# Attention beside the plain passes, last w1's factors, half loads and staging moved in a fused attention and mixture-of-experts kernel

## The chip, the cores and the metric

The kernel runs on one core of one Trainium2 chip. The metric is the device time of one execution in microseconds (us); for a kernel it is the median of its runs. Beside the runs one further execution is profiled, and its trace is what the views of the profile show. In them PE is TensorE (matmuls; PEld its weight loads), DVE is VectorE, ACT is ScalarE, POOL is GpSimd, SP is SyncE, which issues all DMAs here.

## The reference

Inputs are q, k, v of shape (8, 8, 576, 64): batch, heads, sequence, head size. In each chunk of 64 positions softmax attention is computed; the result is the input x of four experts. All is fp32.

```python
scores = scale * np.matmul(q_c, k_c.transpose(0, 1, 2, 4, 3))     # per chunk of 64
attn = np.exp(scores - max); attn = attn / (sum + 1e-09)
x = (attn @ v_c) as (4608 tokens, 512)
p = domain_probs / (domain_probs.sum(-1, keepdims=True) + 1e-09)   # (4608, 4)
for e in range(4):
    h = np.maximum(x @ w1[e], 0.0)       # w1[e]: 512 x 1024
    out += p[:, e:e + 1] * (h @ w2[e])   # w2[e]: 1024 x 512
```

## The kernel before, in words

**Products.** Every fp32 product is three matmuls on parts: a matrix is split into a high part (a cast on ACT, `hi_part` L361) and a low part (what is left, a subtraction on POOL or DVE, `lo_part` L364), and hi x hi, hi x lo, lo x hi are summed in PSUM (`product`, L638). A large matmul is 128 x 128 by 512 columns.

**Passes.** An expert's hidden layer is cut in halves, which gives 8 passes over the weights. The 4608 tokens are a first block of 512 and four pairs of 2 x 512. The first block goes through `startup` (pass 0) and the plain passes 1 to 7; pair 0 through passes 8 to 15, pair 1 through 16 to 23, and so on to 39. A plain pass (`plain_pass`) has 8 steps of 12 matmuls: four hidden steps (`plain_hidden`, its relu on ACT L645 and its low part on DVE L646) and four tiles of the output (`whole`). The last step of pass 7 is held and runs in pass 8.

**Factors.** The passes of the pairs multiply 2 x 2 blocks with seven products instead of eight. Their left factors are the weights' blocks a11, a12, a22 and four sums s1 to s4 (`Factors.sum`, L415), each split into two parts (`make`). The plain passes make the factors of w1 and w2 for the pass they run and store them in DRAM (`keep`, L424 for a sum; `keep_quad`, `keep_unit` for blocks). `w1_split` and `w2_split` split the blocks; these splits the plain products use themselves. The first w1's sums are made in passes 1 to 5 (`FIRST_W1`), the last w1's (that of pass 7) in pass 7 and stored in pass 8. The right factors are x's blocks b11, b21, b22 and sums t1 to t4 (`Tokens`, L588).

**Woven passes.** `first_later_pass` (pass 8) has 14 steps, `later_pass` 28 steps of 6 matmuls in the order of `WOVEN`: a and b are the outer products of the pass before (w2), g and h the hidden ones of this pass (w1), by output half. Products accumulate into banks A, B, C of PSUM; ACT copies one aside (`keep`, L701), DVE adds (L836, and L863 into the output sums `acc`). The relu times the probability is on DVE (L801), sums of the hidden parts on DVE and POOL (L807), the casts and low parts on ACT (L813) and POOL (L816). Each product reads a unit of factors, which `ring_load` brings from DRAM into one of the tiles `wf0` to `wf5` (L536) three units ahead (`ring_next`).

**Factors made later.** For w1 of passes 9 to 14 the stored units don't exist yet when pair 0 needs them: `half_load` (L484) loads half of a w1's raw columns into `xraw`, `half_sum` (L489, DVE) forms s1 to s4 there, and `make` casts on ACT (L501), subtracts on POOL (L502) straight into the ring tile and stores the unit for the later pairs (L505). The places of the makes in a pass are `MAKE_AT`. For the last w2 (used in passes 15 and 16) the sums are formed in pass 7 and stored raw (`keep_sums`); `raw_load` (L525) brings a unit of raw blocks or sums back into the one tile `v_in`, and `make` works from there.

**Attention.** Pair 0's attention (8 tiles of 128 tokens, five steps each, one more to begin) runs beside the plain passes: `Beside.go` is called in each step and issues attention steps at a rate of 41 over 37 per step, so that sometimes two come in one. A tile is: scores on PE (L161), less the maximum (DVE), exp (ACT L243), sums and scaling (DVE), transposes (DVE), copies that place the weights (ACT L194, and four small L198), products with v (PE L208), copies into `xraw` (ACT L223, L224). Pair 1's attention is placed by `TILES` into passes 9 to 14, at the steps `EARLY` and `LATE`: weights, place, values.

**Order.** The kernel fixes the order by hand: each engine works through its instructions in the order in which the program issues them. `add(at, i, f)` puts f behind step i of the pass; `first` is a list issued ahead of `at` in the same step. SP issues DMAs in the same way, and a DMA that has to wait holds those behind it.

## Time and profile before

| quantity | value |
|---|---|
| median of 3 runs | 1523.31 us (1521.61 to 1524.45) |
| the profiled execution | 1522.23 us |
| its span, first to last instruction | 1520.5 us |
| TensorE clock granted, mean over the span | 0.995 |
| instructions | 23324 |
| DMA bytes | 345.89 MB, mean 227 GB/s |

How to read it: the page gives each engine's busy time and share of the span. A row of the timeline has the start and the length in us, the engine, the line, the operation, what is written and read (buffer numbers left out), and in brackets the idle time before it with what ended it. A row of the waits reads: the waiting engine, tile and line, the releaser, then the sum in us, the count and the longest. A row of the windows gives, for a stretch of the span, each engine's busy time with its instructions in brackets, then the granted clock (1.00 is full speed). SPq is SP's queue of DMA issues.

### The profile page before, as it was taken

To read this page: it belongs to the slowest core of one execution; us is meant where nothing else is said; L and a number is where in the kernel's file an instruction comes from. 1 tells how busy PE (TensorE), PEld (TensorE's weight loads), DVE (VectorE), ACT (ScalarE), POOL (GpSimd) and SP (SyncE) were. 2 spreads that over 40 slices of the span, in tenths; PEclk is the share of its full clock that TensorE was granted. 3 is DMA by queue.
4 is the path that set the end of the run, shared out by engine and by line. 5 is a ranking of instruction groups with operands and counts; after the bars stand their busy time and mean duration, and the time that the engine had idled before them with its cause. 6 is when DMAs were issued, how large, how long until landed. Compare 5 with 4: busy or idle time off the path is not lost.

```text
span 1520.5 us, 23324 instructions
## 1 busy us (share of the span) xinstructions
PE 1475.2 (97%) x8556; PEld 1203.5 (79%) x8556; DVE 1081.8 (71%) x1500; ACT 626.2 (41%) x1165; POOL 964.6 (63%) x720
## 2 busy tenths in 40 slices
PE   8999997999999989999999999999999999999998
PEld 7777876777777867888888888888888888888887
DVE  5566664778887786777776886777777966666665
ACT  4546633545445343434343434343343433333332
POOL 4656995777777776555555765555557655555554
PEclk9999999999999999999999999999999999999999
DMA  8778876776766758866666678666665696565655
GB/s 300 243 237 299 305 263 241 237 255 229 249 212 232 271 192 235 277 206 232 213 216 199 200 222 258 229 209 228 209 200 192 199 252 210 193 208 193 207 194 152
DMA packets 199010, 345.89 MB, mean 227 GB/s; under 512 B 69984, under 2 KB 111216, under 8 KB 198000
## 3 DMA queue, kind: packets, MB, share of 16 engines
q1 hardware_dynamic: 198896, 344.40, 68.8%
q8 instruction: 68, 1.11, 0.3%
q14 instruction: 46, 0.38, 0.1%
HBM read 272.97 MB, written 71.38 MB: 226 GB/s over the span
## 4 chain that ended last, share of the span: by engine, by line
PE 61%; DMA 1%; DVE 0%; ACT 0%; POOL 0%; SPq 0%; issue 0%; DVEq 0%; ACTq 0%
PE A L638 34%; PE C L638 17%; PE B L638 8%; PE psa L208 1%; PE psa L161 1%; DMA out<-pt 0%; DMA v_in<-w_sums 0%; DVE acc L863 0%; DVE wraw L807 0%; ACT pt L198 0%; POOL wf L502 0%; POOL hf L816 0%; DVE pt L971 0%; PE C L1596 0%; PE psa L638 0%
## 5 line engine op out<-in xcount | busy, mean ns | idle before, releaser
L816 POOL TENSOR_TENSOR hf<-wraw,hf 128x512 fp32r<-128x512 f32 x384 | 506.6, 1334 | 247.3 <-ACT hf L813 245.0
L638 PE MATMUL A<-hf,wf 128*128 128x512 f32 x1536 | 394.5, 392 | 14.1 <-DMA wf<-w 5.4
L638 PE MATMUL A<-xh,wf 128*128 128x512 f32 (+1 forms) x1104 | 382.3, 390 | 3.8 <-ACT s L701 3.2
L813 ACT CAST hf<-wraw 128x512 fp32r<-128x512 f32 x384 | 234.7, 622 | 303.8 <-DVE wraw L807 99.5
L638 PEld LDWEIGHTS A<-hf,wf 128*128 128x128 f32 x1536 | 286.4, 188 | 80.8 <-DVE acc L863 11.1
L638 PEld LDWEIGHTS A<-xh,wf 128*128 128x128 f32 x1104 | 207.3, 188 | 48.9 <-ACT s L701 4.1
L701 ACT COPY s<-A 128x512 f32<-128x512 f32 x192 | 112.9, 588 | 279.2 <-PE A L638 278.9
L638 PE MATMUL A<-xl,wf 128*128 128x512 f32 (+1 forms) x552 | 214.2, 389 | 0.0
L863 DVE TENSOR_TENSOR acc<-A,acc 128x512 f32<-128x512 f32 x232 | 158.0, 681 | 76.1 <-PE A L638 75.2
L638 PE MATMUL C<-xh,wf 128*128 128x512 f32 (+1 forms) x600 | 205.7, 390 | 3.6 <-DVE B L836 2.9
L638 PE MATMUL C<-hf,wf 128*128 128x512 f32 x768 | 195.1, 389 | 1.0 <-POOL wf L502 0.6
L638 PEld LDWEIGHTS C<-hf,wf 128*128 128x128 f32 x768 | 144.0, 188 | 31.6 <-POOL wf L502 1.1
L807 POOL TENSOR_TENSOR wf<-wraw,wf 128x512 f32<-128x512 f32 x31 | 40.1, 1293 | 155.9 <-DVE wf L801 155.9
L638 PEld LDWEIGHTS C<-xh,wf 128*128 128x128 f32 x600 | 111.5, 188 | 28.7 <-DVE B L836 4.2
L638 PE MATMUL B<-xh,wf 128*128 128x512 f32 (+1 forms) x376 | 124.8, 383 | 0.0
L863 DVE TENSOR_TENSOR acc<-C,acc 128x512 f32<-128x512 f32 x120 | 82.7, 689 | 53.6 <-PE C L638 44.0
L638 PEld LDWEIGHTS A<-xl,wf 128*128 128x128 f32 x552 | 103.8, 188 | 21.1
L638 PE MATMUL C<-xl,wf 128*128 128x512 f32 (+1 forms) x300 | 114.7, 386 | 0.0
L816 POOL TENSOR_TENSOR hf<-wf,hf 128x512 fp32r<-128x512 f32 x64 | 91.9, 1436 | 33.7 <-ACT hf L813 33.3
L807 DVE TENSOR_TENSOR wraw<-wf,wraw 128x512 f32<-128x512 f32 x64 | 92.7, 1448 | 10.2 <-POOL hf L816 9.0
L638 PE MATMUL B<-hf,wf 128*128 128x512 f32 x384 | 97.7, 389 | 0.8 <-POOL hf L816 0.8
L807 POOL TENSOR_TENSOR wraw<-wraw 128x512 f32<-128x512 f32 x64 | 91.9, 1437 | 0.0
(175 smaller groups left out, 1951.3 us busy)
## 6 DMA issues: line engine op xcount, KB each, us to landing
wf<-w SPq DMA_DIRECT2D x399, 512.0 KB, 4.2
w<-wf SPq DMA_DIRECT2D x49, 512.0 KB, 3.0
qk_in<-in_qk SPq DMA_DIRECT2D x32, 512.0 KB, 4.8
w<-hf SPq DMA_DIRECT2D x28, 512.0 KB, 5.8
w<-hf SPq DMA_DIRECT2D x50, 256.0 KB, 5.4
hf<-in_w SPq DMA_DIRECT2D x7, 1024.0 KB, 5.5
wf<-in_w SPq DMA_DIRECT2D x12, 512.0 KB, 7.6
ws<-p_t SPq DMA_DIRECT2D x24, 256.0 KB, 4.1
```

The lines of the kernel that those rows point to most:

```text
L161: nc.tensor.matmul(s["sc"][of_half(half), c, slot], lhsT=q, rhs=k, start=True, stop=True)
L208: nc.tensor.matmul(av[of_half(slot % 2), half, head // 2], lhsT=s["v"][of_half(half), head], rhs=s["pt"][of_half(half), c, slot], start=Tr ...
L638: nc.tensor.matmul(out, lhsT=lhs(k, a), rhs=rhs(k, b), start=first and i == 0, stop=last and i == len(parts) - 1, skip_group_check=not (fi ...
L701: nc.scalar.copy(out=t, in_=self.a)
L807: (eng or nc.vector).tensor_tensor(out=self.values[place, k], in0=self.values[a, k], in1=self.values[b, k], op=op)
L813: nc.scalar.copy(out=self.part(name, 0)[:, k], in_=self.values[name, k])
L816: (eng or nc.gpsimd).tensor_tensor(out=self.part(name, 1)[:, k], in0=self.values[name, k], in1=self.part(name, 0)[:, k].bitcast(F32), op=A ...
L863: nc.vector.tensor_tensor(out=acc[key], in0=src, in1=acc[key], op=ALU.add)
```

## The change

- **Attention beside the plain passes.** `go` issues one attention step per plain step; the second of all comes ahead of the last tile of the startup.
- **Last w1.** Its raw blocks are loaded in pass 1 into `xh4` and `xl4`, which hold x's parts later; its sums are formed on DVE in passes 3 and 4, its factors made in passes 4 and 5 and stored in 5 and 6 (`EARLY_W1`, which also moves the first w1's by up to a pass). Pass 7 makes and pass 8 stores nothing of it.
- **Pass 1 to 7.** w2's splits come one step later, its sums at steps 3, 3, 4, 5, its load at step 6. Of pass 6's four w2 factors two are made in pass 7. x's sums and parts, before in passes 5 to 7, are spread otherwise over them; sum t4 and its low part go from DVE to POOL, in pass 7.
- **Half loads and half sums.** The first half load for pass 9 goes out in pass 7 (before in pass 8), the second in step 9 of pass 8; in passes 9 to 13 they go out at steps 5, 13 and 19 instead of 10 and 18. Half sums move with them. One make moves from step 9 to step 10.
- **Staging.** The raw units of the last w2 are staged in four buffers in turn (`v_in`, `e`, `pt`, and `s4`, which the probabilities used alone), first in first out.

The diff, cut to its core:

```diff
-    def half_load(n, g):
+    def half_load(n, g, fs=(0, 1)):
...
+        for f in fs:
...
-        src = staged.pop() if i else pieces(2 * k, 2)
+        src = staged.pop(0) if i else pieces(2 * k, 2)
...
-    def raw_load():
-        k, t = unstaged.pop(0), load.tile([P, 2, 2, P], F32, name="v_in")
+    def raw_load(pool, name):
+        k, t = unstaged.pop(0), pool.tile([P, 2, 2, P], F32, name=name)
...
-        def __init__(self, pair, n, close):
+        def __init__(self, pair, close):
             self.steps = attention(pair, close)
-            self.rate, self.due = (5 * PAIR * NT + 1) / n, 0.5
-        def load(self):
+        def go(self):
             next(self.steps, None)
-        def go(self):
-            self.due += self.rate
-            while self.due >= 1.0:
-                self.due -= 1.0
-                next(self.steps, None)
...
-        add(at, 2, lambda: w2f[n - 1].keep(1))
+        add(at, 4 if last_pass else 2, lambda: w2f[n - 1].keep(1))
         for i, (k, f) in enumerate(QUADS):
-            add(at, i // 2, lambda f=f, k=k: w2_split(f, k))
+            add(at, 1 + i // 2, lambda f=f, k=k: w2_split(f, k))
         if n == 2:
             add(at, 1, probs_by_expert)
             add(at, 5, transpose_probs)
         add(at, 0, lambda: w2_factors(n))
+        for i, f in EARLY_W1.get(n, ()):
+            add(at, i, f)
         if not last_pass:
+            near = n == n_pass - 2
             add(at, 0, lambda: w1_load(n + 1))
-            for name, i, eng in zip(SUMS, (1, 2 if n == n_pass - 2 else 3, 3, 4), SUMS_ON.get(n, (v,) * 4)):
+            for name, i, eng in zip(SUMS, (3, 3, 4, 5), (v, g, g, g) if near else (v,) * 4):
                 add(at, i, w2_do("sum", name, eng))
             for i, quad in enumerate(KEPT):
-                add(at, 3 + i // 2, lambda quad=quad: keep_quad(n, *quad))
+                add(at, 4 + i // 2, lambda quad=quad: keep_quad(n, *quad))
             for i, (f, k) in enumerate(QUADS):
                 add(at, (3, 4, 4, 5)[i], lambda f=f, k=k: w1_split(f, k, g))
-            for name, i in zip(("s1", "s2", "s4", "s3"), (4, 5, 6, 7)):
+            for name, i in zip(("s1", "s2", "s4", "s3")[: 2 if near else 4], (6, 7) if near else (4, 5, 6, 7)):
                 add(at, i, w2_do("make", name))
-            add(at, 5, lambda: w2_load(n + 1))
-            for i, f in FIRST_W1.get(n, ()):
-                add(at, i, f)
+            add(at, 6, lambda: w2_load(n + 1))
             if n == n_pass - 3:
-                add(at, 5, lambda: xs.append(Tokens(0)), x("sum1"))
-                add(at, 6, x("sum3"))
-                add(at, 6, x("hi", "t1"))
-                add(at, 7, x("lo", "t1"))
-            if n == n_pass - 2:
-                add(at, 0, x("hi", "b22"))
-                add(at, 0, x("lo", "b22"))
-                add(at, 3, x("sum2"), x("hi", "t3"))
-                add(at, 4, x("lo", "t3"), x("hi", "t2"))
-                add(at, 5, x("lo", "t2"))
-                add(at, 6, x("sum4"))
-                add(at, 7, x("hi", "t4"))
+                add(at, 7, lambda: xs.append(Tokens(0)), x("sum1"))
+            if near:
+                add(at, 0, x("sum3"), x("hi", "t1"))
+                add(at, 3, x("lo", "t1"), x("hi", "b22"))
+                add(at, 4, x("lo", "b22"))
+                add(at, 5, x("sum2"), x("hi", "t3"))
+                add(at, 6, x("lo", "t3"))
+                add(at, 7, x("hi", "t2"))
             issue(steps, at, beside, True)
             return None
-        w1f = Factors(0, n, {
-            name: lambda: wpool.tile([P, 2, 2 * P], F32, name="wraw", bufs=N_RAW) for name in ("s1", "s2")
-        })
-        last_w1.append(w1f)
-        places = []
-        def place(i):
-            if i % 2 == 0:
-                places.append(hf_tile(3 + 3 * (i // 2), (2, 2, *UNIT[1:])))
-            return places[-1][:, i % 2]
-        def w1_make(i, name):
-            return lambda: w1f.make(name, place(i))
         add(at, 0, *(lambda quad=quad: keep_unit(n, *quad) for quad in KEPT))
-        add(at, 0, lambda: w1f.sum("s1", v), lambda: w1f.sum("s2", v))
-        add(at, 1, x("lo", "t4"))
-        add(at, 2, w1_make(0, "s1"), w1_make(1, "s2"))
-        add(at, 3, x("hi", "b11"), x("lo", "b11"), lambda: w1f.sum("s3", v))
-        for name, i in zip(SUMS, (2, 2, 3, 3)):
+        add(at, 0, x("lo", "t2"))
+        for name in ("s4", "s3"):
+            add(at, 2, lambda name=name: w2f[n - 1].make(name))
+        for name, i in zip(SUMS, (2, 2, 5, 6)):
             add(at, i, w2_do("sum", name, g))
-        add(at, 4, x("hi", "b21"), x("lo", "b21"), lambda: w1f.sum("s4", v))
-        add(at, 5, w1_make(2, "s3"), w1_make(3, "s4"))
+        add(at, 3, x("hi", "b11"), x("lo", "b11"))
+        add(at, 3, x("sum4", g))
+        add(at, 4, x("hi", "b21"), x("lo", "b21"))
+        add(at, 4, x("hi", "t4"), x("lo", "t4", g))
         for r, i in ((2, 2), (0, 3), (1, 3), (5, 5), (3, 6), (4, 6)):
             add(at, i, lambda r=r: ring_load(0, r, (RINGS[0] + RINGS[1])[r]))
-        add(at, 4, lambda: probs_load(n + 1, 0), lambda: probs_load(n + 1, 1))
-        add(at, 6, w2_do("keep_sums"))
-        add(at, 6, lambda: first_load(1))
+        add(at, 5, lambda: probs_load(n + 1, 0), lambda: probs_load(n + 1, 1))
+        add(at, 6, lambda: first_load(1), w2_do("keep_sums"), lambda: half_load(n + 2, 0))
         issue(steps[:-1], at, beside, True)
...
+    def last_begin():
+        for k, name in enumerate(("xh4", "xl4")):
+            t = xpool.tile([P, 2, HF], F32, name=name)
+            nc.sync.dma_start(out=t, in_=of_pass(w1, n_pass - 1)[:, 2 * k : 2 * k + 2])
+            for f in range(2):
+                raw[0, f, k] = t[:, :, f * 2 * P : (f + 1) * 2 * P]
+        last_w1.append(Factors(0, n_pass - 1, sums_tile("xh3")))
...
+    EARLY_W1 = {
+        1: [(6, early_sum(first_w1, "s1")), (7, early_sum(first_w1, "s2")), (6, last_begin)],
         2: [
+            (6, early_sum(first_w1, "s3")), (7, early_sum(first_w1, "s4")),
+            (7, early_make(first_w1, "s1", "xl2")),
         ],
+        3: [
+            (0, early(first_w1, "keep", "s1")), (6, early_sum(last_w1, "s1")), (7, early_sum(last_w1, "s2")),
+            (6, early_make(first_w1, "s2", "xh6")), (7, early_make(first_w1, "s3", "xl6")),
+        ],
+        4: [
+            (0, early(first_w1, "keep", "s2")), (1, early(first_w1, "keep", "s3")),
+            (6, early_sum(last_w1, "s3")), (7, early_sum(last_w1, "s4")),
+            (6, early_make(first_w1, "s4", "xh5")), (7, early_make(last_w1, "s1", "xl3")),
+        ],
+        5: [
+            (0, early(first_w1, "keep", "s4")), (1, early(last_w1, "keep", "s1")),
+            (5, early_make(last_w1, "s2", "xl5")), (6, early_make(last_w1, "s3", "xl2")),
+            (7, early_make(last_w1, "s4", "xh6")),
+        ],
+        6: [
+            (0, early(last_w1, "keep", "s2")), (0, early(last_w1, "keep", "s3")),
+            (1, early(last_w1, "keep", "s4")),
+        ],
...
-        add(at, 0, lambda: half_load(n + 1, 0), lambda: half_load(n + 1, 1))
-        for name in ("s1", "s2"):
-            add(at, 0, lambda name=name: last_w1[0].keep(name))
-        for name in ("s3", "s4"):
-            add(at, 2, lambda name=name: last_w1[0].keep(name))
-        half_sums(at, 0, (4, 4, 6, 6))
+        add(at, 9, lambda: half_load(n + 1, 1))
+        half_sums(at, 0, (6, 7, 8))
         add(at, 6, lambda: make_next(0))
+        add(at, 10, lambda: make_next(0))
...
-    MAKE_AT = 2, 9, 11, 14, 17, 20, 24
+    MAKE_AT = 2, 10, 11, 14, 17, 20, 24
...
-            add(at, 10, lambda: half_load(n + 1, 0))
-            add(at, 18, lambda: half_load(n + 1, 1))
-            half_sums(at, 0, (15, 16, 22, 22))
-            half_sums(at, 1, (22, 24))
+            add(at, 5, lambda: half_load(n + 1, 0))
+            add(at, 13, lambda: half_load(n + 1, 1, (0,)))
+            add(at, 19, lambda: half_load(n + 1, 1, (1,)))
+            half_sums(at, 0, (15, 15, 22, 22))
         if n_pass < n < 2 * n_pass - 1:
-            places = zip(SUMS, (9, 9, 10, 10)) if n == n_pass + 1 else (("s3", 9), ("s4", 10))
-            for name, i in places:
-                first.setdefault(i, []).append(lambda name=name: half_sum(1, name))
-            for i in (0, 3, *MAKE_AT[1:]) if n == n_pass + 1 else MAKE_AT:
-                first.setdefault(i, []).append(lambda: make_next(0))
+            half_sums(first, 1, (9, 9, 10, 12))
+            if n == n_pass + 1:
+                half_sums(first, 0, (None, None, None, 3))
+            for i in MAKE_AT:
+                add(first if i == 24 else at, i, lambda: make_next(0))
         for m, makes, raws in (
-            (2 * n_pass - 1, (22, 26), (19, 23, 27)), (2 * n_pass, (2, 8, 12, 15, 20), (4, 9, 13, 16)),
+            (2 * n_pass - 1, (20, 27), ((8, load, "v_in"), (22, att, "e"), (23, att, "pt"), (24, load, "v_in"))),
+            (2 * n_pass, (2, 10, 12, 17, 20), ((1, hpool, "s4"), (12, load, "v_in"), (13, hpool, "s4"))),
         ):
             if n == m:
                 for i in makes:
-                    first.setdefault(i, []).append(lambda: make_next(1))
-                for i in raws:
-                    add(at, i, raw_load)
+                    add(at, i, lambda: make_next(1))
+                for i, *place in raws:
+                    add(at, i, lambda place=place: raw_load(*place))
...
-        beside = Beside(0, (n_pass - 4) * 2 * NK + 5, True)
+        beside = Beside(0, True)
```

Where instructions stand, at three places. First ScalarE at the start of plain pass 1, before: `hf_614` is the raw w2, `A`, `B` and the first `hf` are the hidden step's bank and parts, `psa` and `pt` belong to the attention.

```order
L645 ACTIVATE hf_748<-A_749 128x512
L361 CAST hf_766<-hf_614 128x2x256 x2
L645 ACTIVATE hf_748<-A_778 128x512
L243 ACTIVATE psa<-psa 128x2x256
L361 CAST hf_794<-hf_614 128x2x256 x2
L645 ACTIVATE hf_807<-B_808 128x512
L645 ACTIVATE hf_807<-B_826 128x512
L194 COPY pt<-psa 128x512
L198 COPY pt<-psa 32x8x32 x4
```

The same place after, where all lines of the code stand four lower:

```order
L641 ACTIVATE hf_751<-A_752 128x512
L243 ACTIVATE psa<-psa 128x2x256
L641 ACTIVATE hf_751<-A_780 128x512
L357 CAST hf_796<-hf_614 128x2x256 x2
L641 ACTIVATE hf_801<-B_802 128x512
L194 COPY pt<-psa 128x512
L198 COPY pt<-psa 32x8x32 x4
L357 CAST hf_825<-hf_614 128x2x256 x2
L641 ACTIVATE hf_801<-B_830 128x512
```

The four casts that split w2 stand one relu later, and the copies that place the weights stand a relu earlier, now ahead of the second pair of casts.

Second SyncE in pass 8, before: `w_0_k` is a unit of w1's factors in DRAM, `w_1_k` one of w2's, `hf_2362` and `hf_2437` hold the last w1's factors, `wf` is a ring tile.

```order
L424 DMA w_0_1_196<-hf_2362 128x512
L424 DMA w_0_4_199<-hf_2362 128x512
L536 DMA wf_2494<-w_0_6_103 128x1024
L939 DMA out<-acc_527 128x512
L424 DMA w_0_2_197<-hf_2437 128x512
L424 DMA w_0_5_200<-hf_2437 128x512
L424 DMA w_0_3_198<-hf_2437 128x512
L424 DMA w_0_6_201<-hf_2437 128x512
L505 DMA w_0_0_111<-wf_2574 128x1024
L536 DMA wf_2584<-w_1_0_104 128x1024
```

After, from the last store of the w2 sums on:

```order
L464 DMA w_sums<-acc_2466 128x512
L480 DMA xraw<-in_w 128x4x128 x2
L532 DMA wf_2497<-w_0_6_103 128x1024
L935 DMA out<-acc_527 128x512
L501 DMA w_0_0_111<-wf_2570 128x1024
L532 DMA wf_2580<-w_1_0_104 128x1024
L532 DMA wf_2605<-w_1_1_105 128x1024
L480 DMA xraw<-in_w 128x4x128 x2
```

The eight stores of the last w1 are gone from here. Before, both half loads stood ahead of the first row shown; now the first stands behind the w2 sums, still in pass 7, and the second behind w2's second unit (`w_1_1`).

Third ScalarE in pass 10, around step 9, before: `wf` from `xraw` is a make's cast, `s` a product copied aside.

```order
L701 COPY s_3202<-A_3104 128x512
L501 CAST wf_3208<-xraw 128x2x256
L194 COPY pt<-psa 128x512
L198 COPY pt<-psa 32x8x32 x4
L501 CAST wf_3238<-xraw 128x2x256
L223 COPY xraw<-psa 128x2x2x64
L224 COPY xraw<-psa 128x2x2x64
L243 ACTIVATE psa<-psa 128x2x256
```

After:

```order
L697 COPY s_3203<-A_3103 128x512
L194 COPY pt<-psa 128x512
L198 COPY pt<-psa 32x8x32 x4
L497 CAST wf_3226<-xraw 128x2x256
L223 COPY xraw<-psa 128x2x2x64
L224 COPY xraw<-psa 128x2x2x64
L497 CAST wf_3273<-xraw 128x2x256
L243 ACTIVATE psa<-psa 128x2x256
```

Each of the two makes stands behind the attention's copies that it stood ahead of.

65 lines of the change are left out of this document (27 added, 38 removed).

## The prediction

> **What bounds the kernel now.** I read the page first, then the busy time by stage, then TensorE's waits stage by stage, then the rows around each wait. The page:
>
> ```profile
> span 1520.5 us, 23324 instructions
> PE 1475.2 (97%) x8556; PEld 1203.5 (79%) x8556; DVE 1081.8 (71%) x1500; ACT 626.2 (41%) x1165; POOL 964.6 (63%) x720
> ```
>
> TensorE (PE) is the bound and idles 45.3 us, so only idle time, or matmuls that run slowly, can be won. The change adds and drops no matmul. Where the idle time lies, by stage (us of the stretch, then busy time of each engine):
>
> ```profile
> core 0: us, PE busy (x) PEld busy (x) DVE busy (x) ACT busy (x) POOL busy (x), PEclk, DMA share, GB/s
> 0.00:44.00 44.00, 40.05 (x458) 32.76 (x462) 23.04 (x45) 19.32 (x38) 23.27 (x24) 1.00 0.73 259
> 44.00:196.00 152.00, 144.63 (x1076) 117.87 (x1068) 98.84 (x136) 84.14 (x171) 107.23 (x78) 0.98 0.78 273
> 196.00:219.00 23.00, 19.85 (x86) 15.80 (x85) 15.96 (x14) 9.51 (x15) 22.92 (x15) 1.00 0.80 298
> 219.00:252.00 33.00, 25.30 (x99) 20.15 (x98) 14.51 (x21) 9.18 (x16) 16.66 (x14) 0.90 0.88 299
> 252.00:512.00 260.00, 249.78 (x1542) 199.98 (x1541) 202.11 (x297) 121.79 (x235) 196.94 (x147) 1.00 0.69 233
> 512.00:597.00 85.00, 77.71 (x332) 61.16 (x331) 67.17 (x80) 33.75 (x56) 62.06 (x44) 1.00 0.72 227
> 597.00:1520.50 923.50, 917.91 (x4982) 755.81 (x4980) 660.21 (x911) 348.48 (x636) 535.54 (x404) 1.00 0.67 212
> ```
>
> The stages are: start, plain passes 1 to 6, plain pass 7, pass 8 with the head of 9, passes 9 to 14, passes 15 and 16, and the rest. PE idles 3.95, 7.37, 3.15, 7.70, 10.22, 7.29 and 5.59 us in them. The first and the last are not touched. The five between hold 35.73 us, and each of them is edited.
>
> **Plain passes 1 to 6 (7.37 us).** ScalarE (ACT) and PE:
>
> ```profile
> PE psa L208 <- ACT pt L198: 6.4, 4, 2.7
> ...
> 55.45 0.60 ACT L645 ACTIVATE hf<-B 128x512 fp32r<-128x512 f32 x1 [2.06 <-PE B L638]
> ...
> 56.56 1.49 ACT L198 COPY pt<-psa 32x256 f32<-32x256 f32 x4
> ...
> 58.10 0.69 PE L208 MATMUL psa<-pt,v_in 64*64 64x64 f32 x32 [2.68 <-ACT pt L198]
> ...
> 59.24 5.74 PE L638 MATMUL C<-hf,hf 128*128 128x512 f32 x24
> ...
> 229.91 0.39 PE L638 MATMUL B<-xh,wf 128*128 128x512 f32 x1
> ...
> 231.27 0.39 PE L638 MATMUL C<-xh,wf 128*128 128x512 f32 x1
> ```
>
> The copies that place the weights come behind a step's relu, and the value products are wanted at once, since `go` sometimes takes two attention steps. Relu and copies take 2.6 us (55.45 to 58.05). Six matmuls run in 1.36 us (229.91 to 231.27), so a plain step of twelve takes 2.72. With one attention step per step an empty plain step always lies between, so the copies end about when they are wanted. Four of the eight tiles (passes 1, 3, 4, 5) are placed behind a relu: I take 0.1 us each; the others are placed behind steps without one. The split of w2 comes a step later. In pass 1 it stands behind the copies: relu and copies from 8.2 us into the pass (three steps) to 10.8, a cast of 0.6 and two POOL halves of 1.3 (rows of both below), so 14.0. The eighth matmul of the first whole tile wants it at 13.6 (four steps, seven matmuls, and the 1.1 us of an attention step, 58.10 to 59.24): 0.4 us; pass 3 likewise 0.1. The remaining 1.0 us is this, with what the idle time brings behind it:
>
> ```profile
> 86.18 0.50 PE L638 MATMUL A<-hf,hf 128*128 128x512 f32 x1 [1.00 <-DVE hf L646]
> 88.95 1.13 PE L208 MATMUL psa<-pt,v_in 64*64 64x64 f32 x32 [2.27 <-ACT pt L198]
> 90.93 4.74 PE L638 MATMUL A<-hf,hf 128*128 128x512 f32 x12
> ```
>
> VectorE (DVE) had w2's first sum at step 1 of pass 2 beside the copy of the probabilities; it moves to step 3, so I take nothing for it. Together 0.9 us stay, between 0.2 and 3.2 (half of the 6.4).
>
> The twelve matmuls at 90.93 take 4.74 us where twelve take 2.72, and the small ones of an attention step 2.0 (88.95 to 90.93) where 58.10 to 59.24 shows 1.1: the half clock costs about 2.7 us here. [...]
>
> **Plain pass 7 (3.15 us).** POOL is busy 22.92 of 23.00 us there, and PE waits for it:
>
> ```profile
> 208.88 1.66 PE L638 MATMUL A<-hf,hf 128*128 128x512 f32 x6 [1.35 <-POOL hf L364]
> ...
> 186.70 1.30 POOL L415 TENSOR_TENSOR acc<-acc,hf 128x512 f32<-128x512 f32 x1
> 187.96 2.28 POOL L415 TENSOR_TENSOR acc<-hf 128x512 f32<-128x512 f32 x1
> ...
> 186.82 2.26 DVE L588 TENSOR_TENSOR xraw<-xraw,qk_in 128x1024 f32<-128x1024 f32 x1
> ```
>
> The four factors of the last w1 leave POOL in pass 7, two w2 factors of pass 6 come instead, behind the splits. After the change pass 6 has 13 POOL operations. From 6.6 us on (two steps, a relu and a cast), at 1.3 us and with 5 us for five wide DVE operations beside them (2.28 instead of 1.30), they end 28.5 us after that pass began, 6.7 us into pass 7 (a pass is 8 x 2.72). Four splits and one more microsecond of that contention end at 12.9; the eighth matmul of the first whole tile is due at 12.5. POOL has nothing left to give way with, so I take 0.9 us and not 0.4, between 0 and 3.15.
>
> **Pass 8 and the head of 9 (7.70 us).**
>
> ```profile
> 239.16 0.50 PE L638 MATMUL A<-xh,wf 128*128 128x512 f32 x1 [2.29 <-ACT s L701]
> 246.23 2.90 PE L638 MATMUL A<-hf,wf 128*128 128x512 f32 x6 [5.41 <-DMA wf<-w]
> 251.48 0.48 PE L638 MATMUL C<-xh,wf 128*128 128x512 f32 x1
> ...
> 225.34 5.50 SPq L484 DMA_DIRECT2D xraw<-in_w  x4
> 230.89 3.59 SPq L424 DMA_DIRECT2D w<-hf  x4
> 234.57 0.56 SPq L536 DMA_DIRECT2D wf<-w  x1
> ...
> 235.92 2.85 SPq L424 DMA_DIRECT2D w<-hf  x4
> 238.86 0.74 SPq L505 DMA_DIRECT2D w<-wf  x1
> 239.69 2.43 SPq L536 DMA_DIRECT2D wf<-w  x3
> ...
> DMA to landing us min/median/max: 3.1/4.2/8.4
> ```
>
> SyncE (SP) needs 6.4 us to issue eight stores of the last w1's factors; they go to passes 5 and 6. The load of w2's first unit, issued last (239.69), lands at 246.1. The last row is of all loads L536. After the change, in us from the start of pass 7: POOL works from 6.7 on, 14 times 1.3 us (an operation of double width counts twice) and 4 us of contention, so its last w2 sum ends at 29; half a load of w1 issues at 30 and lands near 33.5; cast and POOL half until 35.4; the store, and behind it the unit's load at 35.9; landing 3.1 to 4.2 later, 39.0 to 40.1. PE wants it at 38.9 (19.9 for seven steps with the wait above, a held tile 2.72, twelve steps of 1.36). I take 1.2 us, and 0.3 for the last half of x that POOL makes there. ACT's cast of the first half load stood ahead of the copy that PE waits for; it now finds its load landed, so the 2.29 go. 1.5 us stay, between 0 and 5.5. The half clock (12 matmuls in 5.25 us, 246.23 to 251.48, that take 2.72) costs 2.5 us and goes with the long gap.
>
> **Passes 9 to 14 (10.22 us).**
>
> ```profile
> 311.52 0.62 ACT L501 CAST wf<-xraw 128x512 fp32r<-128x512 f32 x1
> ...
> 314.21 0.69 PE L208 MATMUL psa<-pt,v_in 64*64 64x64 f32 x32 [0.49 <-ACT pt L198]
> ...
> PE C L638 <- DVE B L836: 2.9, 3, 1.4
> ...
> DVE xraw L489 <- DMA xraw<-in_w: 9.1, 4, 3.8
> ```
>
> Five value products wait about 0.5 us each, about the length of the cast ahead of the copies (311.52). The cast moves behind them (steps 9 to 10): these 2.6 us go. But the unit is used at step 12: cast at 313.6, after copies of 2.1 us, POOL 0.7 later and 1.3 long, 315.6, against 315.3 for the third matmul of g3, which reads it (314.21 less the 0.49, an attention step of 1.1, two matmuls): 0.3 us, five times. The half loads go out five steps earlier (6.8 us) and DVE waited 3.8 us at most for one: PE's waits behind them (the 2.9 and smaller ones) shrink to 0.5, and those for ACT at the head of pass 9 to 0.2. 2.2 us stay, between 0.8 and 5.5.
>
> **Passes 15 and 16 (7.29 us).**
>
> ```profile
> ACT wf L501 <- DMA v_in<-w_sums: 17.6, 4, 5.6
> ```
>
> One staging buffer means that each load starts after the last cast. With four, every load has at least five steps (6.8 us) ahead of its cast, over the longest wait of 5.6 us. ACT's queue, with the keeps and casts behind the cast, is free. What stays is DVE's x halves in pass 15: 1.0 us, between 0.4 and 3.
>
> **The sum.** Idle 35.73 becomes 0.9 + 0.9 + 1.5 + 2.2 + 1.0 = 6.5, and 5.2 us of half clock go: 1522.23 (the profiled execution, 1.7 over its span) - 29.2 - 5.2 = 1487.8. The median of the runs lies 1.1 above that execution: 1489. With the low ends (1.4 us) 1484; with the high ends (20.4 us) and one half-clock stretch kept, 1505.
>
> **Rivals.** First, POOL takes PE's place: with PE no longer waiting elsewhere, its chain through passes 6 to 9 sets the pace, so 3.15 and 7.70 us stay, half of 10.22, and 1.9 in the other two stages: 17.9 us idle, and one half-clock stretch of 2.5 with them: 1522.23 - 17.8 - 2.7 + 1.1 = 1503. For it: 22.92 of 23.00 us. Against: in the stage after, 16.66 of 33. [...] Chance 0.20.
>
> Second, the cast at step 10 finds POOL busy with an operation of 1.3 us: five passes, 6.5 us, 1495. Chance 0.08.
>
> Third, slower: SP works in order, and the half loads now stand ahead of w2's loads, waiting for POOL's halves of the units whose place they take.
>
> ```profile
> SPq L505 <- POOL wf L502: 161.4, 43, 9.4
> ```
>
> SP waits so already, up to 9.4 us, and PE waited for a load once. There are 15 such places in passes 9 to 13. It decides if each makes a load late by over 2.3 us (15 x 2.3 = 34.5); at 2.5 us the time is 1527. Chance 0.02.
>
> Fourth, it doesn't do what it says: each freed wait meets the next one a little later, and the time stays at 1523. Against it stand 923 us at the end with 5.59 us idle, in passes with the same woven order but no factors to make. Chance 0.03.
>
> **The numbers.** My forecast has 0.67. The range 1482 to 1505 takes in its bounds, with 1.7 below since single runs of before lie up to 1.7 under their median, the first rival and the second. Differences under 0.2% (3 us) can't be told from none here. Faster: 0.67 + 0.20 + 0.08 = 0.95; same 0.03; slower 0.02.
>
> **What would show it.** The same stages in the new profile: no PE wait over 1 us in passes 1 to 6 and no clock under 1.00 there; no DMA wait of ACT's casts in 15 and 16; small waits for POOL in pass 7 and at g3. It is wrong if POOL is the releaser of waits of 5 us and more between 196 and 260 us, or if waits for loads appear in passes 9 to 14.

## The result and the profile after

The changed kernel takes 1497.2 us (median of 4 runs, 1496.92 to 1498.45), the kernel before 1523.2. The ratio is 0.9831, with a 95% interval of 0.9814 to 0.9849: 26 us faster, where 34 had been forecast. First the page of the profile after:

```profile
span 1495.5 us, 23335 instructions
PE 1472.0 (98%) x8556; PEld 1198.9 (80%) x8556; DVE 1091.8 (73%) x1500; ACT 625.5 (42%) x1165; POOL 971.7 (65%) x720
```

PE's idle time fell from 45.3 to 23.5 us, and its busy time by 3.2 us at the same 8556 matmuls. To compare stages, a pass is now taken from the end of its first hidden product to the end of the next pass's, in both kernels. The rows are passes 1 to 6, pass 7, pass 8, passes 9 to 14, 15 and 16, and the rest; the first fence is before, the second after.

```profile
47.26:199.14 151.88, 144.51 (x1059) 117.78 (x1059) 99.18 (x136) 85.03 (x171) 107.68 (x77) 0.98 0.79 277
199.14:220.55 21.41, 18.26 (x80) 14.49 (x79) 15.96 (x14) 8.62 (x14) 21.33 (x15) 1.00 0.81 297
220.55:254.50 33.95, 26.25 (x103) 20.90 (x103) 15.48 (x22) 9.80 (x17) 17.27 (x13) 0.90 0.85 292
254.50:509.67 255.17, 244.95 (x1521) 196.03 (x1521) 198.10 (x292) 120.06 (x232) 193.73 (x144) 1.00 0.68 233
509.67:596.02 86.35, 79.06 (x337) 62.29 (x337) 68.52 (x82) 33.97 (x56) 62.14 (x44) 1.00 0.72 228
596.02:1520.50 924.48, 918.89 (x4987) 756.59 (x4985) 661.15 (x912) 349.37 (x637) 536.52 (x404) 1.00 0.67 213
```

```profile
47.24:192.81 145.57, 142.85 (x1059) 115.48 (x1059) 100.88 (x138) 85.19 (x172) 111.78 (x79) 1.00 0.85 296
192.81:211.71 18.90, 18.25 (x80) 14.50 (x79) 9.65 (x10) 7.28 (x12) 17.94 (x12) 1.00 0.90 317
211.71:239.17 27.46, 23.84 (x103) 18.91 (x103) 15.80 (x21) 10.83 (x18) 18.62 (x14) 1.00 0.89 320
239.17:492.07 252.90, 246.71 (x1522) 195.12 (x1521) 210.97 (x293) 119.64 (x232) 197.97 (x145) 1.00 0.71 237
492.07:572.58 80.51, 78.13 (x338) 62.55 (x337) 68.36 (x82) 34.08 (x56) 63.26 (x44) 1.00 0.76 241
572.58:1495.50 922.92, 918.74 (x4986) 756.86 (x4985) 661.44 (x912) 349.14 (x637) 536.17 (x404) 1.00 0.67 213
```

PE's busy time fell by 1.7 us in passes 1 to 6 and by 2.4 in pass 8, where the granted clock rose from 0.98 and 0.90 to 1.00: that is the half clock, 0.50 before from 87.8 to 94.7 us and from 244.8 to 251.7, and gone in this execution. In passes 9 to 14 it rose by 1.8 us at a clock of 1.00. The lengths give, against the forecast's terms (idle and half clock together):

| passes | forecast | measured |
|---|---|---|
| 1 to 6 | -9.2 | -6.3 |
| 7 | -2.3 | -2.5 |
| 8, head of 9 | -8.7 | -6.5 |
| 9 to 14 | -8.0 | -2.3 |
| 15 and 16 | -6.3 | -5.8 |
| start and rest | 0 | -1.6 |

So the miss lies in passes 9 to 14, then in 1 to 6 and 8. The largest waits of PE that are left there, from the timeline:

```profile
82.97 0.50 PE L634 MATMUL A<-hf,hf 128*128 128x512 f32 x1 [0.83 <-POOL hf L360]
...
164.01 0.50 PE L208 MATMUL psa<-pt,v_in 64*64 64x64 f32 x17 [0.78 <-ACT pt L198]
...
219.34 0.50 PE L634 MATMUL C<-xh,wf 128*128 128x512 f32 x1 [2.18 <-DVE acc L931]
...
233.32 0.47 PE L634 MATMUL A<-hf,wf 128*128 128x512 f32 x1 [1.44 <-DMA wf<-w]
...
252.29 0.50 PE L634 MATMUL A<-hf,wf 128*128 128x512 f32 x1 [1.37 <-ACT acc L857]
...
308.14 0.74 PE L634 MATMUL A<-hf,wf 128*128 128x512 f32 x2 [0.42 <-DVE acc L859]
```

The last one returns in each of passes 10 to 13; what is at 219 and 308 was not in the forecast. Three theories for the missing 8 us followed. **T1:** in pass 8 the waits at 219 and 233 are one cost, since w2's first unit lands when it lands. **T2:** in passes 10 to 13 two half sums on VectorE, side by side in step 15, run beside GpSimd and delay an output sum. **T3:** the wait at 252 is GpSimd's chain. The rival to all three is the forecast's first: GpSimd paces everything, and what one place gives the next takes.

### The profile page after: what moved, and what is told of

Same layout as the page of the kernel before. It is cut to its first block, busy times and chain, and to the rows that moved or that the text cites. A ratio compares the mean times of both kernels' runs of the same rounds, so it can differ in the third digit from the quotient of the medians.

```text
span 1495.5 us, 23335 instructions
## 1 busy us (share of the span) xinstructions
PE 1472.0 (98%) x8556; PEld 1198.9 (80%) x8556; DVE 1091.8 (73%) x1500; ACT 625.5 (42%) x1165; POOL 971.7 (65%) x720
## 4 chain that ended last, share of the span: by engine, by line
PE 76%; POOL 8%; DVE 6%; DMA 4%; issue 3%; ACT 2%; SPq 1%; POOLq 0%; ACTq 0%; DVEq 0%
PE A L634 40%; PE C L634 22%; PE B L634 11%; POOL hf L812 4%; POOL wf L498 2%; DVE xraw L485 2%; DMA xraw<-in_w 1%; POOL wraw L803 1%; PE psa L208 1%; POOL hf L360 1%; PE psa L161 1%; DMA wf<-w 1%; DMA v_in<-in_v 1%; DVE acc L859 1%; DVE wraw L803 1%
```

## Experiments

Behind the first two rows, all are edits of the changed kernel, except the one that says so. The time is the ratio to the kernel before, measured in the same rounds, times 1523.2; by that measure the changed kernel itself is at 1497.5. The lengths are of one profiled execution each.

An interval is some 5 us wide, so two rows under about 4 us apart can't be told apart by their times alone; there the lengths have to decide. Of these, pass 8 needs care. Six other rows have the code of after in pass 8 (old rate, one staging buffer, old half loads, make in step 9, make ahead, half sum in step 16), and it takes 28.3 to 29.1 us in them against 27.5 in after. PE waits 2.05 to 2.87 us at the matmul of 219 in them (2.18 in after), and the granted clock over the 3 to 4 us behind that wait was 0.56 to 0.69 in the six and 1.00 in after. So after shows pass 8 at its luckiest.

| kernel | ratio (95%) | us | 1-6 | 7 | 8 | 9-14 | 15-16 |
|---|---|---|---|---|---|---|---|
| before | 1 | 1523.2 | 151.9 | 21.4 | 33.9 | 255.2 | 86.4 |
| after | 0.9831 (0.9814-0.9849) | 1497.5 | 145.6 | 18.9 | 27.5 | 252.9 | 80.5 |
| old rate | 0.9863 (0.9849-0.9878) | 1502.3 | 151.0 | 18.9 | 28.3 | 253.0 | 79.9 |
| one staging buffer | 0.9871 (0.9851-0.9892) | 1503.6 | 145.7 | 18.7 | 28.8 | 252.9 | 87.0 |
| old half loads | 0.9865 (0.9844-0.9887) | 1502.6 | 145.6 | 18.7 | 28.4 | 258.3 | 81.5 |
| make in step 9 | 0.9828 (0.9808-0.9847) | 1497.0 | 145.7 | 18.6 | 28.7 | 252.7 | 81.0 |
| make ahead | 0.9834 (0.9817-0.9850) | 1497.9 | 145.8 | 18.8 | 29.1 | 252.8 | 80.7 |
| before, late stores | 0.9945 (0.9927-0.9964) | 1514.8 | 152.0 | 23.0 | 25.7 | 256.6 | 86.5 |
| probabilities earlier | 0.9833 (0.9819-0.9848) | 1497.8 | 145.6 | 18.8 | 29.4 | 252.0 | 80.7 |
| and half load first | 0.9808 (0.9794-0.9823) | 1494.0 | 145.6 | 18.6 | 26.6 | 252.0 | 80.0 |
| and late w2 sums | 0.9807 (0.9788-0.9827) | 1493.8 | 145.7 | 18.8 | 26.2 | 252.9 | 81.5 |
| half sum in step 16 | 0.9814 (0.9797-0.9830) | 1494.9 | 145.7 | 18.8 | 29.1 | 249.9 | 81.2 |
| combined | 0.9786 (0.9766-0.9807) | 1490.6 | 145.6 | 18.6 | 27.5 | 247.6 | 79.8 |
| combined, late w2 sums | 0.9783 (0.9766-0.9801) | 1490.1 | 145.6 | 18.7 | 25.6 | 248.4 | 80.5 |

### What each part of the change was worth

**The rate of the attention** (`rate` is 41/37, and the startup's second step is dropped).

```diff
-            next(self.steps, None)
+            self.due += self.rate
+            while self.due >= 1.0:
+                self.due -= 1.0
+                next(self.steps, None)
```

> Undoes one part: attention beside the plain passes again at 41 steps over 37 plain steps, with two attention steps in some plain steps, and only one in the startup. Theory A (the rate is what removed the waits for the weights' copies in passes 1 to 5): waits of 2 to 2.7 us come back at two tiles, with one stretch at half clock of some 2.5 us, so 6 to 9 us slower, 1503 to 1506. Theory B (the shift of w2's splits and sums does most of it): 1 to 3 us slower, 1498 to 1500, and no clock under 1.00 in these passes.

Measured: passes 1 to 6 are 5.4 us longer, the time 4.8 us, which lies between the two theories. Of the 5.4 us, 4.0 are idle time; the rest is busy time, with the granted clock at 0.73 behind the wait at the first tile. That wait is back as it was:

```profile
58.09 0.60 PE L208 MATMUL psa<-pt,v_in 64*64 64x64 f32 x12 [2.68 <-ACT pt L198]
...
88.63 0.69 PE L208 MATMUL psa<-pt,v_in 64*64 64x64 f32 x32 [0.72 <-ACT pt L198]
```

The one in pass 2, 2.27 us before, is only 0.72. Another part of the change won the rest of it; the shift of w2's splits and sums is the likely one, but no run undoes it alone. So the rate is the larger part of 6.3 us, not all.

**Staging in four buffers.**

```diff
-  ((8, load, "v_in"), (22, att, "e"), (23, att, "pt"), (24, load, "v_in"))
+  ((19, load, "v_in"), (23, load, "v_in"), (27, load, "v_in"))
-  ((1, hpool, "s4"), (12, load, "v_in"), (13, hpool, "s4"))
+  ((4, load, "v_in"), (9, load, "v_in"), (13, load, "v_in"), (16, load, "v_in"))
```

(the makes at their former steps too)

> Undoes one part: the raw units of the last w2 staged in the one buffer v_in again, with the loads and makes at their former steps. Theory A (the single buffer made ScalarE's casts wait for loads, and TensorE behind them): the four waits of 5.6 us at most come back on ScalarE, pass 16 takes 46.8 us instead of 41.0, and the time rises by 5 to 6 us, to about 1503. Theory B (what fell in passes 15 and 16 came from the half loads and sums before them): within 1 us of after's 1497.2.

Measured: 6.1 us slower by the ratio, and passes 15 and 16 are 6.5 us longer. (The start, 49.1 us instead of 47.2 and at a clock of 0.66 from 10 to 20 us, and pass 8 are longer in this execution too; no edit is there.) ScalarE's waits in this run, and the one that is left after:

```profile
ACT wf L497 <- DMA v_in<-w_sums: 18.1, 4, 6.3
```

```profile
ACT wf L497 <- DMA v_in<-w_sums: 1.8, 1, 1.8
```

Theory A holds, and with it that term of the forecast. The run puts the makes back together with the buffer, so the two are not separated.

**Half loads far ahead.**

```diff
-            add(at, 5, lambda: half_load(n + 1, 0))
-            add(at, 13, lambda: half_load(n + 1, 1, (0,)))
-            add(at, 19, lambda: half_load(n + 1, 1, (1,)))
-            half_sums(at, 0, (15, 15, 22, 22))
+            add(at, 10, lambda: half_load(n + 1, 0))
+            add(at, 18, lambda: half_load(n + 1, 1))
+            half_sums(at, 0, (15, 16, 22, 22))
+            half_sums(at, 1, (22, 24))
```

(and the sums of `first` at 9 and 10)

> Undoes one part: in passes 9 to 13 the half loads at steps 10 and 18 again, and the half sums at their former steps (the make stays at step 10). Theory A (early half loads won what they were meant to, and the two half sums in step 15 gave it back): TensorE's waits of 1.4 to 1.5 us behind VectorE in passes 9 and 12 come back (about 3.3 us with 1 us for smaller ones), the four of 0.7 us behind the half sums go (2.8 us): within 1 us of 1497.2. Theory B (the early loads are worth what the forecast took): 4 to 5 us slower, 1501 to 1502.

Measured: 5.1 us slower, 5.4 of it in passes 9 to 14. By size that is theory B; but passes 9 to 14 are then 3.2 us longer than before the change. With the old loads beside the rest of the change, PE waits behind VectorE in every pass of 9 to 13 (three such waits before, of up to 1.4 us):

```profile
PE C L634 <- DVE B L832: 4.4, 5, 1.0
```

So the loads are worth 5.4 us only beside the other edits; the parts don't add up, and no run shows which of the other edits makes the old loads cost more.

**The make behind the copies.** Step 9 alone first:

```diff
-    MAKE_AT = 2, 10, 11, 14, 17, 20, 24
+    MAKE_AT = 2, 9, 11, 14, 17, 20, 24
```

> After, with one edit undone: the make of step 10 in passes 9 to 14 in step 9 again, where its cast stands ahead of the copies that place the weights. Theory A (the term of the forecast): five value products wait 0.5 us more each, and the third matmul of g3 no longer waits for GpSimd (0.3 to 0.4 us each): 0.5 to 1 us slower, 1498. Theory B (GpSimd's half of that unit ends late anyway, because GpSimd is slowed by VectorE's half sums beside it): the waits at g3 stay and the value products' come back, 2.5 to 3 us slower, 1500.

Nothing changed at these places, and neither theory was tested: in step 9 the attention is put in `at` first, so the cast stays behind its copies. What the change really did was to take the makes out of `first`. The proper undoing:

```diff
-                add(first if i == 24 else at, i, lambda: make_next(0))
+                add(first if i in (9, 24) else at, i, lambda: make_next(0))
```

> After, with the make of step 10 in step 9 again and issued ahead of the attention's copies there, as it was before the change. (In the run before, step 9 alone left the cast behind the copies in ScalarE's order, and nothing at these places changed.) Theory A (the term of the forecast): TensorE loses 0.65 to 0.7 us at each of five value products again, the waits of 0.3 us at the third matmul of g3 go, and passes 10 to 13 get 0.2 to 0.4 us longer each, so 0.5 to 1.5 us slower in all, 1498 to 1499. Theory B (VectorE's half sums of step 15 start earlier and find GpSimd free, so the wait of 0.58 us behind them goes too): 1 to 2 us faster, 1495 to 1496.

Measured: passes 9 to 14 as long as after (252.8 against 252.9), the time within the intervals. The waits of the value products are back and those at g3 gone, as theory A had it, but they balance. This run's waits stand first, those of after second. Their sums don't balance, because much of the wait at g3 is booked as busy time; the starts of the matmuls do: 0.5 us lost at each of five value products here, against 0.4 at g3 in each of passes 10 to 13 and 0.9 in pass 14 in after.

```profile
PE psa L208 <- ACT pt L198: 3.7, 7, 0.8
...
PE C L634 <- POOL wf L498: 0.6, 1, 0.6
```

```profile
PE psa L208 <- ACT pt L198: 1.2, 2, 0.8
...
PE C L634 <- POOL wf L498: 1.1, 2, 0.6
```

The forecast had 1.1 us of gain for this edit (2.6 less 1.5); it is worth nothing that these runs can tell.

**The eight stores of the last w1**, in the kernel before:

```diff
-        for name in ("s1", "s2"):
-            add(at, 0, lambda name=name: last_w1[0].keep(name))
-        for name in ("s3", "s4"):
-            add(at, 2, lambda name=name: last_w1[0].keep(name))
+        for name in ("s1", "s2", "s3", "s4"):
+            add(at, 9, lambda name=name: last_w1[0].keep(name))
```

> The kernel before, with one edit: the eight stores of the last w1's factors go out after step 9 of pass 8, behind the first loads of w2's units, and not after steps 0 and 2. Theory A (these stores, 6.4 us of SyncE's queue, made the first w2 unit late): its load is issued at about 236 and not at 239.7, TensorE's wait of 5.41 us shrinks to about 2 and the half clock behind it (2.5 us) goes: 3 to 6 us faster than before's 1523.2, so 1517 to 1520. Theory B (the unit is late because the half load, issued at 225, is cast at 233.9, and GpSimd is busy): within 1 us of 1523.2.

Measured: 8.4 us faster than before by the ratio, with an interval of 5.5 to 11.1, and 5.1 by the spans of the two profiled executions; so 3 to 6 us were a fair estimate, and more is not shown. Pass 8 takes 25.7 us instead of 33.9. (Pass 7, without an edit, takes 1.6 us longer in this execution, at a clock of 0.82 to 0.90, and passes 9 to 14 take 1.4 longer.) SyncE in this run, and the matmul that waited 5.41 us for the unit before:

```profile
236.38 1.21 SPq L536 DMA_DIRECT2D wf<-w  x2
237.64 6.40 SPq L424 DMA_DIRECT2D w<-hf  x8
```

```profile
242.12 1.16 PE L638 MATMUL A<-hf,wf 128*128 128x512 f32 x4 [1.25 <-DVE wraw L807]
```

The unit's load leaves at 236.4 and not at 239.7, and the wait for it is gone. Theory A holds: in the kernel before, stores that nobody waits for stood in a queue ahead of a load that everybody waits for. The loads also land sooner after their issue: the first half load in 6.7 us instead of 8.5, the unit in 5.6 instead of 6.4. With that the wait at 239, for which ScalarE stood behind the cast of the half load, fell from 2.29 to 0.72 us. So the stores cost time in SyncE's queue and, it seems, on the DMA engines; this run doesn't separate the two.

### What stood in the way

**T1, pass 8.** VectorE and SyncE after:

```profile
217.93 0.69 DVE L797 SCALAR_TENSOR_TENSOR wraw<-B,ws 128x512 f32<-128x512 f32 x1 [2.92 <-DMA ws<-p_t]
218.54 0.74 DVE L931 SCALAR_TENSOR_TENSOR acc<-C,pr,acc 128x512 f32<-128x512 f32 x1
```

```profile
210.54 1.43 SPq L1353 DMA_DIRECT2D ws<-p_t  x2
...
215.05 4.03 SPq L464 DMA_DIRECT2D w_sums<-acc  x4
219.24 1.76 SPq L480 DMA_DIRECT2D xraw<-in_w  x2
```

The probabilities, issued at 210.54, are late; VectorE waits for them until 217.9, and behind it in order stands the held tile's sum, for whose bank PE waits until 219.34. The change had moved their loads by a step; so:

```diff
-        add(at, 5, lambda: probs_load(n + 1, 0), lambda: probs_load(n + 1, 1))
+        add(at, 4, lambda: probs_load(n + 1, 0), lambda: probs_load(n + 1, 1))
```

> Undoes one edit: the two loads of the probabilities go out after step 4 of pass 7 instead of step 5. In the trace of after, VectorE waits 2.92 us for such a load (ws<-p_t) at 217.9, the held tile's sum L931 stands behind it, and TensorE waits 2.18 us for that sum at 219.34. Theory A (this load was late and its wait is a cost of its own): the wait goes and the time falls by about 2.3 us, from 1497.2 to 1494.9. Theory B (the first w2 unit, for which TensorE waits 1.44 us at 233.32, lands at a time of its own, set by the half load behind the stores of the w2 sums): the wait at 219 goes, the one at 233 grows to about 3.7, and the time stays at 1497.2 within 0.6 us.

The wait at 219 went, and the time didn't move. Theory B: the next waits took it all, one for w1's last unit and one for w2's first. PE idles 3.8 us in pass 8, as it did in after (3.6).

```profile
220.69 0.50 PE L634 MATMUL A<-xh,wf 128*128 128x512 f32 x1 [0.72 <-DMA wf<-w]
...
233.60 0.47 PE L634 MATMUL A<-hf,wf 128*128 128x512 f32 x1 [3.05 <-DMA wf<-w]
```

The unit's load follows the half load, and the half load follows four stores. With those turned too:

```diff
-        add(at, 6, lambda: first_load(1), w2_do("keep_sums"), lambda: half_load(n + 2, 0))
+        add(at, 6, lambda: first_load(1), lambda: half_load(n + 2, 0), w2_do("keep_sums"))
```

> As the run before (probabilities after step 4), and the first half load of w1 ahead of the four stores of the w2 sums instead of behind them. In after SyncE issues these stores from 215.05 to 219.08 and the half load at 219.24; its scratch is free when GpSimd has made the low part of t4 (216.27). Theory B: the half load goes out 3 us earlier, so the first w2 unit lands 3 us earlier, both waits go, and the time falls by 3.3 to 3.7 us to about 1493.7. Theory A: 1494.9 as in the run before, since the unit was not what held TensorE. A third way: GpSimd, busy 20.61 of 23 us in the stage before, makes the half unit no earlier, and the time is as in the run before.

3.5 us faster than after by the ratio, 2.5 by the span; the intervals allow either. The run before, measured in the same rounds, is the better measure: 1494.7 us against 1498.6, with no run of the one within the range of the other. Of these 3.9 us, 2.8 lie in pass 8: 1.2 are idle time, and the rest goes with the clock, which was 0.63 behind the wait at 233 in the run before and is 1.00 here. The direction is T1's, the size at this place isn't: the half load left 3.0 us earlier but took 7.9 us to land instead of 7.2, the unit's load left 2.2 us earlier (at 226.67, in after at 228.87), and the unit landed only 1.0 earlier.

```profile
226.67 1.57 SPq L532 DMA_DIRECT2D wf<-w  x2
```

```profile
232.32 0.47 PE L634 MATMUL A<-hf,wf 128*128 128x512 f32 x1 [1.71 <-DMA wf<-w]
```

Are the DMA engines full? The w2 sums' stores out of the way:

```diff
-        add(at, 6, lambda: first_load(1), lambda: half_load(n + 2, 0), w2_do("keep_sums"))
+        add(at, 6, lambda: first_load(1), lambda: half_load(n + 2, 0))
# first_later_pass
+        add(at, 10, w2f[n - 1].keep_sums)
```

> After, with the probabilities' loads after step 4 of pass 7 (as in two runs before) and the four stores of the w2 sums (256 KB each) in step 10 of pass 8, behind the second half load. In the run with only the order of half load and stores turned, the load of w2's first unit went out at 227.06, 2.2 us earlier than in after, but landed 5.2 us later instead of 4.0, with the DMA engines' share at 1.02 to 1.07 from 204 to 228 us. Theory A (the DMA engines are full there, and 1 MB of stores ahead of the half load and the unit is what makes them land late): the unit lands at 230 to 231, TensorE's wait of 1.71 us for it goes, and the time is 1.5 to 2 us under that run's 1494.7, so about 1493. Theory B (GpSimd's chain to the half unit sets it): 1494.7 within 0.6 us.

The unit lands 1.0 us earlier, close to where theory A had it, and the total doesn't move, as theory B had it: another load is late instead. The half load, with no stores ahead of it, still takes 8.5 us to land, with the DMA engines' share at 1.03 from 212 to 220 us; so the stores are not what makes it slow.

```profile
220.92 0.50 PE L634 MATMUL A<-xh,wf 128*128 128x512 f32 x1 [1.65 <-DMA wf<-w]
...
231.33 0.47 PE L634 MATMUL A<-hf,wf 128*128 128x512 f32 x1 [0.54 <-DMA wf<-w]
```

**T2, the half sums.** VectorE and GpSimd after, in pass 10:

```profile
305.33 2.15 DVE L485 TENSOR_TENSOR xraw<-xraw 128x256 f32<-128x256 f32 x2
307.41 0.68 DVE L859 TENSOR_TENSOR acc<-A,acc 128x512 f32<-128x512 f32 x1
```

```profile
304.47 1.30 POOL L498 TENSOR_TENSOR wf<-xraw,wf 128x512 fp32r<-128x512 f32 x1 [1.95 <-ACT wf L497]
305.74 2.88 POOL L812 TENSOR_TENSOR hf<-wraw,hf 128x512 fp32r<-128x512 f32 x2
```

```diff
-            half_sums(at, 0, (15, 15, 22, 22))
+            half_sums(at, 0, (15, 16, 22, 22))
```

> Undoes one edit: the second half sum of the passes 9 to 13 back from step 15 to step 16. In after two half sums take 2.15 us of VectorE (305.33 in pass 10) beside GpSimd's make, ahead of the output sum L859 that frees TensorE's bank; TensorE loses 0.58 us there and 0.11 more in weight loads, in each of passes 10 to 13, and nothing at this place in before. Theory A: this place costs 4 x 0.7, the time falls by 2.8 us to 1494.4. Theory B: VectorE is late anyway at step 18 and the wait moves to the next output sum: 1497.2 within 0.6 us.

Passes 9 to 14 take 249.9 us instead of 252.9, and the time falls by 2.6: theory A, by the length of the stage, since 2.6 us are within the intervals. The output sum now stands between the two half sums:

```profile
306.30 0.72 DVE L485 TENSOR_TENSOR xraw<-xraw 128x256 f32<-128x256 f32 x1
306.94 0.68 DVE L859 TENSOR_TENSOR acc<-A,acc 128x512 f32<-128x512 f32 x1
307.54 0.92 DVE L485 TENSOR_TENSOR xraw<-xraw 128x256 f32<-128x256 f32 x1
```

**T3, and all together.** ScalarE and GpSimd at the head of pass 9, after:

```profile
251.14 0.62 ACT L809 CAST hf<-wraw 128x512 fp32r<-128x512 f32 x1 [5.25 <-POOL wraw L803]
251.66 0.58 ACT L857 COPY acc<-A 128x512 f32<-128x512 f32 x1
```

```diff
# with the edits above, and in pass 7 and at the head of pass 9:
-        add(at, 3, x("sum4", g))
+        add(at, 3, x("sum4"))
-            (4, lambda: sc.sum("t4", 0, nc.gpsimd)),
+            (4, lambda: sc.sum("t4", 0)),
# and t4 of the second half in pass 9 likewise
```

> After, with five edits: the probabilities' loads after step 4, the half load ahead of the w2 sums' stores, the half sum of passes 9 to 13 in step 16, x's sum t4 in pass 7 on VectorE again, and the two sums t4 at the head of pass 9 on VectorE (idle there from 246.2 to 252.3) and not on GpSimd. Theory A (three places of their own: the w2 unit, the half sums, and GpSimd's chain at the head of pass 9, where ScalarE's copy waits 5.25 us for a GpSimd sum and TensorE 1.37 us for that copy): 3.5 + 2.8 + 1.5 us, and about 1 for t4, so 1488 to 1490. Theory B (GpSimd sets the pace of passes 7 to 9, and what one wait gives the next takes): the half sums alone, with the 3.5 us that were measured, 1491 to 1492.

> The combined kernel with the same move of the w2 sums' stores into step 10 of pass 8. There TensorE waited 1.26 us for w1's last unit at 220.92 and 2.49 us for w2's first at 233.23, and nothing above 0.2 us from there to 361 us. Theory A (full DMA engines): both waits shrink to under 1 us together, and the time falls by 2.5 to 3 us from 1492.3 to 1489.5. Theory B: within 0.6 us of 1492.3.

Measured: 1490.6 and 1490.1, 7 us under the changed kernel. The first lies between what its two theories expected (1488 to 1490, 1491 to 1492). The wait at 252 is gone (PE idles 0.15 us in pass 9 of the first instead of 1.87); in all the other edits of after it stayed at 1.3 to 1.4 us. So T3 holds, with one thing open: these runs move three sums from GpSimd to VectorE at once, one in pass 7 and two at the head of pass 9, and don't show which of them it took. In pass 8 the first of the two still waits for loads, the second for less; their totals can't be told apart:

```profile
PE A L634 <- DMA wf<-w: 3.7, 2, 2.5
```

```profile
PE A L634 <- DMA wf<-w: 1.4, 2, 0.9
```

## Why the prediction was right in kind and 8 us too low

- **Passes 1 to 6** (0.9 us of idle time was to stay; 2.7 stayed). The mechanism was right. The term was mis-sized: w2's split is 0.83 us late in pass 2, not 0.4 in pass 1, and two tiles' copies 0.46 and 0.78, not 0.1. Of the half clock 2.7 us were to go; PE's busy time fell by 1.7.
- **Pass 7**: as worked out, 0.65 us of idle time left against 0.9.
- **Pass 8**: the unit's wait, forecast at 1.2 us, was 1.44, but that is luck. Counted from the start of pass 7, the unit landed at 43.3 us and not at 39.0 to 40.1: the half load, issued at 29.3 as forecast, took 7.2 us to land and not 3.5, a term that no row stood behind. And PE came for the unit at 42.0, not at 38.9. The step that failed there is "the 2.29 go": they went, and the probabilities' loads, which the diff moved by a step and I passed over, put 2.18 us in their place. Removing that alone won nothing. That the half clock went is luck too: in six other executions of the same code the clock behind that wait was 0.56 to 0.69. The forecast let its 5.2 us go with the gaps, but the runs don't tie the clock to the length of a gap: behind the same wait of 2.68 us it was 1.00 before and 0.73 with the old rate.
- **Passes 9 to 14** (2.2 was to stay; the stage won 2.3 us and not 8). Three steps failed. The make's edit won nothing, not 1.1. The half sums were taken to cost nothing; two in a row beside GpSimd cost 2.6 to 3.0 us. And the wait at the head of pass 9 (1.16 us before) was to shrink to 0.2, for which the forecast gave no reason; it stayed at 1.37 until GpSimd's sums were moved to VectorE. Short waits also cost more than their idle time: at 308.14, where 0.42 us are booked as idle, the starts of the matmuls show 0.69 lost.
- **Passes 15 and 16**: the mechanism as worked out, with 2.4 us of idle time left, not 1.0. One of ScalarE's casts still waits for a load (1.8 us), where none was to.
- **The rest** gained 1.6 us without an edit in it. Of these, 1.1 lie behind the last matmul, from whose end to the end of the span it takes 4.9 us before and 3.8 after; in make ahead, which has after's code there, it takes 5.0. So that part is scatter between executions.
- **The rivals.** "GpSimd paces passes 6 to 9" was wrong for pass 7, and right at the head of pass 9. For pass 8 its shape was right (one wait takes what another gives), but the carrier was the chain of loads. The second rival didn't come: GpSimd had been idle for 2.68 us when the moved make reached it (296.98 in pass 10). Late w2 loads in 9 to 13 didn't come.

What stays open is why the old half loads cost more beside the other edits than before the change, and which of the three sums held PE at 252.

## What to carry to other kernels

When a wait is removed, look for what is next late at the same product before counting the gain: here two waits in one pass were one cost. In a queue that is worked through in order, as SyncE's here (the unit's load left 3.3 us earlier once the eight stores stood behind it), put stores that nobody waits for behind the loads that somebody does; one such move took 8.4 us (5.5 to 11.1) off the kernel before. And when sums are moved to where their data is early, check which engine works beside them there: two half sums in a row beside GpSimd cost 2.6 to 3.0 us.

## What the runs showed of the hardware

**VectorE beside GpSimd.** A half sum (128x256, both inputs in SBUF) takes 0.41 us alone and up to 1.52 beside GpSimd. The rows are all half sums before, and after (shortest, median and longest in ns):

```profile
L489 DVE TENSOR_TENSOR xraw<-xraw x48: 407/424/1514, 234.7 to 484.4; 128x256 f32<-128x256 f32 x48
```

```profile
L485 DVE TENSOR_TENSOR xraw<-xraw x48: 412/726/1521, 227.6 to 470.4; 128x256 f32<-128x256 f32 x48
```

Of the 48, 21 ran alone before and 13 after, all in 0.41 to 0.43 us; 9 ran wholly beside GpSimd instructions before and 21 after, in 0.72 to 1.52 us. Why they take longer there, no run shows.

**The half clock doesn't follow from the length of a wait.** The same wait of 2.68 us at 58.1 left the clock at 1.00 in the kernel before and at 0.73 with the old rate; the startup, the same code up to 20 us, ran at 1.00 after and at 0.66 in the run with one staging buffer, whose startup takes 1.9 us longer. The windows of these four, in that order:

```profile
58.00:64.00 6.00, 5.90 (x85) 5.02 (x86) 1.70 (x3) 2.87 (x7) 4.69 (x4) 1.00 0.47 139
```

```profile
58.00:64.00 6.00, 5.91 (x79) 5.09 (x80) 0.47 (x2) 2.86 (x7) 3.85 (x4) 0.73 0.41 95
```

```profile
10.00:20.00 10.00, 9.28 (x193) 8.77 (x194) 5.53 (x10) 4.83 (x9) 3.82 (x3) 1.00 1.01 382
```

```profile
10.00:20.00 10.00, 9.32 (x132) 8.96 (x132) 3.77 (x8) 3.76 (x7) 2.54 (x2) 0.66 0.99 377
```

In pass 8 a wait of 2.18 us left it at 1.00 in after, and one of 2.05 us at 0.64 with the old rate.

What decides whether the clock falls, no run shows. By the busy time and the clock behind them (2.59 us at 0.56 in half sum in step 16, from 219 to 222 us; 5.91 at 0.73 with the old rate), waits of 2 to 3 us cost an estimated 1.1 to 1.6 us more in some executions than in others: part of the scatter of these times, and a reason to compare pass by pass.
